# A two-branch linear-attention kernel rebuilt: small folds, V ahead of K, q's softmax in phase 1, tiles in pairs, an order listed by a planner

## The chip, the cores and the metric

One Trainium2 chip, one of its cores, one launch. The metric is device microseconds of an execution; the time is the median of some runs. TensorE (PE in the profile), VectorE (DVE), ScalarE (ACT), GpSimd (POOL) and the DMA queue of SyncE (SP) each work through their own list of instructions in order and wait for each other by semaphores.

## The reference

Two branches, A and B, with weights of their own, take the same x (2048 rows, 448 columns). A branch makes q, k and v for 16 heads of 28, maps q and k by a 28x28 matrix per head, and takes two softmaxes of each map, of the logits and of their negative, side by side. Then comes linear attention without a mask, an output projection, and a gate that mixes the branches:

```python
qkv = (x @ wqkv).reshape(B, S, 3, H, Dh) ...
pq = jnp.einsum("bhsd,hdf->bhsf", q, w_phi)
phi_q = jnp.concatenate([_softmax(pq, axis=-1), _softmax(-pq, axis=-1)], axis=-1)
...
kv = jnp.einsum("bhsf,bhsd->bhfd", phi_k, v)
z  = jnp.einsum("bhsf->bhf", phi_k)
num = jnp.einsum("bhqf,bhfd->bhqd", phi_q, kv)
den = jnp.einsum("bhqf,bhf->bhq", phi_q, z)[..., None] + 1e-6
o = num / den          # then  o @ wo
...
g = _sigmoid((x * gate_w).sum(-1, keepdims=True))
return g * a + (1 - g) * b
```

The two einsums kv and z sum over all rows, so nothing of num can start before the last tile of k.

## The kernel before

The rows are 16 tiles of 128. Every float32 matrix is held as a high and a low part (a rounded copy and the difference), and a product is made of the three terms that matter; that is why a projection of 448 inputs takes 11 matmuls a branch.

**Folds** (`fold`, L130). The map w_phi is multiplied into the weights of k and q at the start, as differences from the last feature, so that 27 columns a head remain and the 28th logit is zero. `fold` makes a chunk of 128 input rows with eight matmuls of 112x128 into a pair of PSUM banks; ACT makes the high part, DVE the low part. K's four chunks stand ahead of everything, q's four are made in tiles 2 to 5.

**Phase 1** (`for t in range(NT)`, L279). Per tile: `proj` of K (22 matmuls), `shift` (L161: DVE takes maximum and minimum of each head, subtracts for both signs; ACT takes the exponentials), `k_soft` (L175: DVE sums, reciprocal, POOL multiplies), `proj` of V (22 matmuls), `v_out` on ACT, and `kv_acc` (L196) of the tile before, 32 small matmuls that add kv and z into one PSUM bank. PSUM tiles of two banks rotate among three buffers (`two_tile`, L123). POOL splits x (L86) and wo (L251).

**The way of q.** `q_front` (L211) subtracts the maximum on DVE and writes the tile to DRAM with four transfers, then reads it back in another layout (32 tokens of four groups on the partitions). `q_exp0`, `q_min`, `q_exp1` (L229 to L239) make both exponentials there, undivided, and `q_turn` (L246) transposes them in blocks of 32 on DVE. q of tiles 0 to 3 goes through at the end of phase 1 and right after it, the rest in phase 2, four tiles ahead.

**The turn.** After phase 1, `kvs` is copied and transposed to `kvt`, wo is loaded into the place of K's weights (L340), and `gates` (L268) sends the last three tiles' gates through DRAM.

**Phase 2** (`for i in range(NT + 2)`, L437), an order written by hand. Per tile: `num` (L361: 64 matmuls of 32x32, the two signs kept apart, with a column of ones for the softmax's sums), q's projection of a later tile, `n_turn` (DVE transposes 2048 columns), `n_rec` and `n_mix` (reciprocals, products, gate and the sum of the signs; POOL, the last two tiles on DVE), `o_turn` (L400) with its low part (L410, L414), `out_mm` (L418: 21 matmuls) and the store. All transfers are issued by SP in the order of the code.

Of the kernel before, what the change touches and what calls it, by code (L numbers as in the profile page):

```python
# [8 lines left out]
F32 = mybir.dt.float32  # L9
# [16 lines left out]
HP = 32  # L26
WARM = 16
LEAD = 4
T0 = NT - 3
MID = 4  # L30


@with_exitstack
def hedgehog_mix(ctx: ExitStack, tc: tile.TileContext, xd, wv, wkt, wqt, wphi, wo, cmask, cpmask, out):
    nc = tc.nc
    ctx.enter_context(tc.manual_schedule())

    const = ctx.enter_context(tc.tile_pool(name="const", bufs=1))
    one_stack = ExitStack()
    one = one_stack.enter_context(tc.tile_pool(name="one", bufs=1, space=bass.MemoryType.PSUM))  # L40
    two_stack = ExitStack()
    two = two_stack.enter_context(tc.tile_pool(name="two", bufs=1, space=bass.MemoryType.PSUM))


    xg = [const.tile([P, 7, GT], F32R, name=f"xg{g}") for g in range(NG)]
    glog = const.tile([P, NT], F32, name="glog")
    gate = const.tile([P, 2, 4, NT], F32, name="gate")
    kvs = const.tile([P, 2, 2, 4, HP], F32, name="kvs")
    kvt = const.tile([P, 2, 2, 4, HP], F32, name="kvt")
    work = ctx.enter_context(tc.tile_pool(name="work", bufs=2))  # L50
    dram = ctx.enter_context(tc.tile_pool(name="dram", bufs=1, space=bass.MemoryType.DRAM))
# [4 lines left out]
    qd = [dram.tile([4, 32, 4, 8 * DH], F32, name=f"qd{i}") for i in range(2)]  # L56
    ph = ctx.enter_context(tc.tile_pool(name="ph", bufs=2))
    wp_ = ctx.enter_context(tc.tile_pool(name="wts", bufs=1))

    res = ctx.enter_context(tc.tile_pool(name="res", bufs=1, side="right"))  # L60
    wtb = res.tile([P, 4096], F32, name="wtb")
    xrb = res.tile([P, 2048], F32, name="xrb")
    start = ExitStack()
    raw = start.enter_context(tc.tile_pool(name="raw", bufs=1, side="right"))
    ident = raw.tile([P, P], F32, name="ident")
    make_identity(nc, ident)
    mask = raw.tile([PF, 4], F32, name="mask")
    wp = raw.tile([PF, 2, 4, HP], F32, name="wp")
    wpd = raw.tile([PF, 2, 4, FD], F32, name="wpd")
    bd = wp_.tile([PF, 2, 4, 4 * FD], F32, name="bd")  # L70
    wkh = wp_.tile([P, 4, 2 * FW], F32R, name="wkh")
    wkl = wp_.tile([P, 4, 2 * FW], F32R, name="wkl")
    wvh = wp_.tile([P, 4, VC], F32R, name="wvh")
    wvl = wp_.tile([P, 4, VC], F32R, name="wvl")
    NV = 2
    vs = [ph.tile([P, 2, NP, 2, DH + 1], F32, name=f"vs{i}", bufs=1) for i in range(NV)]
# [16 lines left out]
    def load_wt(src, n):
        wt = wtb[:PF].rearrange("p (b g c) -> p b g c", b=2, g=4)
        for c in range(0, 512, n):
            for b in range(2):
                nc.sync.dma_start(wt[:, b, :, c:c + n], src[b, :, c:c + n].rearrange("(g p) c -> p g c", p=PF))
        return wt

    def load_wv(c):  # L100
        wvr[c] = raw.tile([P, VC], F32, name=f"wvr{c}")
        nc.sync.dma_start(wvr[c], wv[c * P:(c + 1) * P, :])

    def split_w(wr, wh, wl, eng):
        nc.scalar.activation(wh, wr, AF.Copy)
        eng.tensor_tensor(wl, wr, wh.bitcast(F32), OP.subtract)  # L106

    nc.sync.dma_start(wp, wphi)
    nc.sync.dma_start(mask, cmask)
    wt = load_wt(wkt, 128)  # L110
    load_x(0, 0, P)
    for c in range(4):
        load_wv(c)
    load_x(0, P, 2 * P, GT)
    for v in vs:
        nc.gpsimd.memset(v[:, :, :, :, DH:], 1.0)
    nc.vector.tensor_tensor(wpd, wp[:, :, :, :FD], wp[:, :, :, FD:DH].to_broadcast([PF, 2, 4, FD]), OP.subtract)
    for q in range(4):
        nc.vector.tensor_scalar(bd[:, :, :, q * FD:(q + 1) * FD], wpd, mask[:, q:q + 1], None, op0=OP.mult)
    twos = [two.tile([P, 2, 512], F32, name=f"two{i}") for i in range(3)]  # L120
    turn_of = [0]

    def two_tile():  # L123
        turn_of[0] += 1
        return twos[turn_of[0] % 3]

    for ps in twos:
        nc.vector.memset(ps[:, :, FZ:FZ + H], 0.0)

    def fold(c, wt, wh, wl):  # L130
        ps = two_tile()
        for b in range(2):
            for g in range(4):
                nc.tensor.matmul(ps[:, b, g * 4 * FD:(g + 1) * 4 * FD], wt[:, b, g, c * P:(c + 1) * P], bd[:, b, g],  # L134
                                 start=True, stop=True)
        dh = wh[:, c, :].rearrange("p (b f h) -> p b f h", b=2, f=FD)
        dl = wl[:, c, :].rearrange("p (b f h) -> p b f h", b=2, f=FD)
        src = ps[:, :, :FW].rearrange("p b (h f) -> p b f h", f=FD)
        nc.scalar.activation(dh, src, AF.Copy)
        nc.vector.tensor_tensor(dl, src, dh.bitcast(F32), OP.subtract)  # L140

    def proj(t, wh, wl, widths, ps, at=0):
        x = xg[t // 4]
        o = (t % 4) * P
        lo = 0
        for b, n in enumerate(widths):
            terms = [(c, wh, c) for c in range(3)] + [(4 + c, wh, c) for c in range(3)]
            terms += [(3, wh, 3)] + [(c, wl, c) for c in range(4)]
            for i, (xc, w, wc) in enumerate(terms):
                nc.tensor.matmul(ps[:, b, at:at + n], x[:, xc, o:o + P], w[:, wc, lo:lo + n],  # L150
                                 start=i == 0, stop=i == len(terms) - 1)
            lo += n
        return ps
# [4 lines left out]
    def fm(ps):  # L158
        return ps[:, :, FO:FO + D].rearrange("p b (f h) -> p b h f", h=H)

    def shift(ps):  # L161
        p4 = fm(ps)
        mx = ph.tile([P, 2, 2, H], F32, name="mx")
        e = ph.tile([P, 2, HA * DH], F32, name="e")
        nc.vector.tensor_reduce(mx[:, 0], p4, AX.X, OP.max)  # L165
        nc.vector.tensor_reduce(mx[:, 1], p4, AX.X, OP.min)
        e5 = e.rearrange("p s (b h f) -> p s b h f", b=2, f=DH)
        bc = [mx[:, s, :, :, None].to_broadcast([P, 2, H, DH]) for s in range(2)]
        nc.vector.tensor_tensor(e5[:, 0], p4, bc[0], OP.subtract)  # L169
        nc.vector.tensor_tensor(e5[:, 1], bc[1], p4, OP.subtract)  # L170
        for s in range(2):
            nc.scalar.activation(e[:, s], e[:, s], AF.Exp)  # L172
        return e

    def k_soft(e):  # L175
        sm = ph.tile([P, 2, HA], F32, name="sm")
        rs = ph.tile([P, 2, HA], F32, name="rs")
        for s in range(2):
            nc.vector.tensor_reduce(sm[:, s], e[:, s].rearrange("p (h f) -> p h f", f=DH), AX.X, OP.add)  # L179
# [4 lines left out]
        return e

    def v_out(t, ps):
        v = vs[t % NV]
        nc.scalar.activation(v[:, :, :, :, :DH].rearrange("p b j q f -> p b (j q) f"), hb(ps[:, :, :D]), AF.Copy)
        nc.scalar.activation(glog[:, t:t + 1], ps[:, 0, D:D + 1], AF.Copy)


    kvb = one.tile([P, 512], F32, name="one")
    nc.vector.memset(kvb, 0.0)
    kvp = kvb[:, :HA * DH // 2].rearrange("p (b g s f) -> p b g s f", b=2, g=4, f=DH)

    def kv_acc(t, phi):  # L196
        v = vs[t % NV]
        for b in range(2):
            for g in range(4):
                for r in range(4):  # L200
# [8 lines left out]
    def q_front(k, ps):  # L211
        seq[k] = len(seq) % 2
# [13 lines left out]
    def tview(k):  # L226
        return tq[seq[k]].rearrange("p c b g f -> p (b g) c f")
# [282 lines left out]
```

## Time and profile before

| what | value |
|---|---|
| median of 3 runs | 393.68 us (393.07 to 394.75) |
| the profiled execution | 395.19 us |
| its span, first to last instruction | 393.4 us |
| mean granted PE clock | 0.965 |
| bytes moved by DMA | 38.5 MB |

The profile is of one execution. Busy time counts what an engine spends in instructions; a stage view gives it for stretches of the span. Matmuls are counted by passes, and a plain float32 one has two: 64 matmuls of `num` are 128 records. In a group's row stand the line, the engine, the operation, the output and input, the shapes, the count, then busy us and mean ns of one, then the idle time before them. The chain that ended last is followed back from the last instruction; its rows have start, length and what.

### The profile page before, as it was taken

How to read it: one execution, taken by the hardware profiler on the slowest of the kernel's cores; microseconds unless marked ns; L12 is line 12 of the kernel's file. 1: busy time of each engine (PE TensorE's matmuls, PEld its weight loads, DVE VectorE, ACT ScalarE, POOL GpSimd, SP SyncE). 2: the span in 40 equal slices, each digit the busy share in tenths (PEclk: the TensorE clock that was granted, in tenths of full speed). 3: DMA queues.
4: the chain of work that ended last, by engine and by line, in shares of the span. 5: the costliest groups of instructions: out<-in, count | busy, mean ns of one | idle time of the engine just before them, and what ended most of it. 6: DMA issues, size and time to landing. Idle time of an engine off the chain costs nothing.

```text
span 393.4 us, 10387 instructions
## 1 busy us (share of the span) xinstructions
PE 355.6 (90%) x4608; PEld 320.0 (81%) x4608; DVE 294.4 (75%) x326; ACT 122.8 (31%) x174; POOL 220.7 (56%) x182
## 2 busy tenths in 40 slices
PE   5999999999999999999965179999999999997765
PEld 5999999999999999999963069888888888875554
DVE  2676767666666667669743299999999999998991
ACT  1744353233333333222410032332233333332112
POOL 0184816375444444313400399988888988889311
PEclk9999999999999999999987588999999999999989
DMA  8928411100222222131158133444434334420001
GB/s 183 311 65 271 184 49 56 53 25 26 90 69 68 69 68 69 25 96 47 48 140 351 28 97 93 118 120 118 118 80 149 76 102 121 118 95 25 27 23 47
DMA packets 27217, 38.52 MB, mean 98 GB/s; under 512 B 3732, under 2 KB 21892, under 8 KB 26884
## 3 DMA queue, kind: packets, MB, share of 16 engines
q1 hardware_dynamic: 27172, 37.85, 31.9%
q8 instruction: 36, 0.59, 0.6%
q14 instruction: 9, 0.07, 0.1%
HBM read 23.62 MB, written 15.84 MB: 100 GB/s over the span
## 4 chain that ended last, share of the span: by engine, by line
PE 71%; DVE 10%; DMA 8%; POOL 4%; issue 2%; SPq 2%; ACT 2%; POOLq 0%; DVEq 0%; ACTq 0%
PE two L150 33%; PE out L423 14%; PE q L150 12%; PE num L367 5%; PE two L134 4%; PE one L203 3%; DMA gd<-glog 3%; POOL xrb L235 2%; DMA tq<-qd 2%; DMA qd<-uq 2%; DVE wtb L247 1%; SPq L223 1%; DVE wvh L373 1%; DVE wvl L373 1%; DVE qmx L216 1%
## 5 line engine op out<-in xcount | busy, mean ns | idle before, releaser
L183 POOL TENSOR_TENSOR e<-e,rs 128x896 f32<-128x896 f32 x32 | 53.9, 1706 | 64.9 <-DVE rs L180 64.9
L423 PE MATMUL out<-wkh,e 128*128 128x448 f32 x224 | 52.4, 372 | 10.9 <-ACT bd L428 6.5
L172 ACT ACTIVATE e<-e 128x896 f32<-128x896 f32 x32 | 30.2, 954 | 97.5 <-DVE e L169 97.4
L423 PEld LDWEIGHTS out<-wkh,e 128*128 128x128 f32 x224 | 41.7, 189 | 16.8 <-ACT bd L428 8.0
L150 PE MATMUL q<-wqh,xg 128*128 128x432 f32 x168 | 41.6, 391 | 13.9 <-DVE uq L218 8.9
L150 PE MATMUL two<-wvh,xg 128*128 128x450 f32 (+1 forms) x224 | 50.8, 365 | 0.0
L150 PE MATMUL two<-wkh,xg 128*128 128x432 f32 x224 | 50.7, 365 | 0.0
L150 PEld LDWEIGHTS q<-wqh,xg 128*128 128x128 f32 x168 | 33.3, 204 | 18.2 <-DVE uq L218 9.4
L165 DVE TENSOR_REDUCE mx<-two 128x32 f32<-128x896 f32 x16 | 17.5, 1091 | 38.2 <-PE two L150 38.2
L150 PEld LDWEIGHTS two<-wvh,xg 128*128 128x128 f32 x224 | 42.1, 188 | 3.2
L150 PEld LDWEIGHTS two<-wkh,xg 128*128 128x128 f32 x224 | 40.9, 188 | 2.9 <-POOL xg L91 0.2
L235 POOL TENSOR_TENSOR xrb<-qmn,tq 128x896 f32<-128x896 f32 x16 | 28.2, 1762 | 23.5 <-DVE qmn L234 19.8
L247 DVE STREAM_TRANSPOSE wtb<-xrb 128x2048 f32<-128x2048 f32 x16 | 36.9, 2305 | 3.1 <-ACT xrb L239 3.1
L367 PE MATMUL num<-wtb,kvt 32*32 32x128 f32 x2048 | 31.6, 285 | 4.9 <-issue 2.5
L367 PEld LDWEIGHTS num<-wtb,kvt 32*32 32x32 f32 x2048 | 25.0, 104 | 11.8 <-issue 7.0
L179 DVE TENSOR_REDUCE sm<-e 128x32 f32<-128x896 f32 x32 | 33.3, 1080 | 1.1
L406 ACT ACTIVATE e<-turn 128x512 fp32r<-128x512 f32 x16 | 9.6, 599 | 69.8 <-DVE turn L403 69.8
L150 PE MATMUL two<-wvl,xg 128*128 128x450 f32 (+1 forms) x128 | 31.3, 365 | 0.0
L150 PE MATMUL two<-wkl,xg 128*128 128x432 f32 x128 | 30.6, 360 | 0.0
L423 PE MATMUL out<-wkl,e 128*128 128x448 f32 x112 | 26.4, 377 | 0.0
L373 DVE STREAM_TRANSPOSE wvh<-num 128x2048 f32<-128x2048 f32 x8 | 18.4, 2306 | 10.4 <-PE num L367 10.4
L150 PEld LDWEIGHTS two<-wvl,xg 128*128 128x128 f32 x128 | 24.0, 188 | 2.3 <-POOL wvl L106 0.4
(95 smaller groups left out, 623.5 us busy)
## 6 DMA issues: line engine op xcount, KB each, us to landing
tq<-qd SPq DMA_DIRECT2D x16, 448.0 KB
qd<-uq SPq DMA_DIRECT2D x36, 112.0 KB
out<-bd SPq DMA_DIRECT2D x16, 224.0 KB
wod<-wtb SPq DMA_DIRECT2D x14, 224.0 KB
qd<-wvh SPq DMA_DIRECT2D x28, 112.0 KB
xrb<-in_xt SPq DMA_DIRECT2D x3, 1024.0 KB
wvr<-in_wv SPq DMA_DIRECT2D x4, 449.0 KB
wtb<-in_wkt SPq DMA_DIRECT2D x8, 224.0 KB
```

What stands on the lines that cost most here:

```text
L134: nc.tensor.matmul(ps[:, b, g * 4 * FD:(g + 1) * 4 * FD], wt[:, b, g, c * P:(c + 1) * P], bd[:, b, g], start=True, stop=True)
L150: nc.tensor.matmul(ps[:, b, at:at + n], x[:, xc, o:o + P], w[:, wc, lo:lo + n], start=i == 0, stop=i == len(terms) - 1)
L165: nc.vector.tensor_reduce(mx[:, 0], p4, AX.X, OP.max)
L172: nc.scalar.activation(e[:, s], e[:, s], AF.Exp)
L179: nc.vector.tensor_reduce(sm[:, s], e[:, s].rearrange("p (h f) -> p h f", f=DH), AX.X, OP.add)
L183: nc.gpsimd.tensor_tensor(e3, e3, rs[:, s, :, None].to_broadcast([P, HA, DH]), OP.mult)
L203: nc.tensor.matmul(kvp[32 * r:32 * r + DH + 1, b, g], v[:, b, h // 2, h % 2], phi[:, :, hs:hs + DH], start=(t == 0 and b == 0 and g == 0), ...
L235: nc.gpsimd.tensor_tensor(eq[:, 1, :, :, :DH], mn.rearrange("p c a -> p a c")[:, :, :, None].to_broadcast([P, 8, 4, DH]), tview(k), OP.sub ...
L247: nc.vector.transpose(e_slot(k), eq.rearrange("p s a c f -> p (s a c f)"))
L367: nc.tensor.matmul(ps[32 * g:32 * g + 32, r, 2 * b + s], kvt[32 * r:32 * r + 32, b, s, g], eTs[i][32 * r:32 * r + 32, s, b, g], start=True ...
L373: nc.vector.transpose(cb[i % 2][:, :2048], ps.rearrange("p r a t -> p (r a t)"))
L423: nc.tensor.matmul(ps[:, :D], a, w, start=n == 0, stop=n == len(terms) - 1)
```

## The change

The kernel is written anew around a planner. `Plan` takes each step with an engine, a cost in us, keys that it reads and writes, and emits the steps in the order of a simulated run: at each moment the engine that is free first takes, among what is ready, the step whose due time is earliest. TensorE's order is that of the list `steps()`. The costs are written into the code; what the chip does with them is not fed back.

- **Folds:** per branch 64 matmuls of 32x32 with 128 columns into all four banks of one PSUM tile, one DVE transpose of 2048 columns, then high and low parts by quarters.
- **Start:** x of two tiles (512 KB) and the first branch's V weights (four pieces of 230 KB) are loaded ahead of K's (eight of 230 KB); V of tiles 0 and 1 is made before the first fold. x comes in pairs of tiles (256 columns), three pairs kept.
- **PSUM:** two tiles of four banks in place of the rotating ones. K has two banks, V two, q two, kv one, each of them single.
- **K's softmax:** DVE subtracts for one sign; ACT copies the logits to SBUF (`pk`) and POOL subtracts for the other. The sums' reciprocals are taken per sign.
- **q's softmax:** `q_soft` sums both exponentials, takes reciprocals and multiplies on POOL before the transpose, through one buffer (`eq`). Tiles 0 to 9 have it in phase 1; tiles 0 to 7 are then kept in DRAM (`spill`, 1 MB each) and read back (`fetch`) in phase 2; tiles 10 to 15 have it in phase 2.
- **num:** with q divided by its sums, the two signs add in PSUM; two tiles share one transpose and one reciprocal. The column of ones is gone.
- **mix:** one product with the gated reciprocal and one for the output, on POOL; the last pair on DVE.
- **Phase 2:** eight pairs of tiles; the out matmuls of a pair follow num of the next.

The diff, cut to its core, added lines only (the old functions they replace are those above):

```diff
+                    f = free.get(eng, 0.0)
+                    if eng == "SP" and len(flight) >= 8:
+                        f = max(f, flight[-8])
+                    t = max(f, min(ready[i] for i in c))
+                    if best is None or t < best[0]:
+                        best = t, eng
+            t, eng = best
+            i = min((i for i in can[eng] if ready[i] <= t), key=lambda i: due[i])
+            can[eng].remove(i)
+            _, cost, lat, _, _, kb = self.steps[i]
...
+    yield from (("V", 0, 0), ("V", 1, 0), ("V", 0, 1), ("FK", 0), ("V", 1, 1), ("FK", 1), ("x1",), ("V", 2), ("x", 2))
+    yield from (("K", 0), ("wq", 0), ("wq", 1), ("FQ", 0), ("V", 3), ("FQ", 1), ("later",), ("K", 1), ("wo_rows",), ("V", 4))
+    yield from (("K", 2), ("Q", 0), ("S", 0, 0), ("kv", 0, 1), ("V", 5), ("K", 3), ("Q", 1), ("S", 1, 1))
+    for p in range(2, 8):
+        if p < 7:
+            yield "x", p + 1
+        yield "K", 2 * p
+        yield "Q", 2 * p - 2
+        if 2 * p - 2 < JIT:
+            yield "S", 2 * p - 2, 0
+        yield "kv", 2 * p - 2, 2 * p - 1
+        yield "wo", p - 2
+        if p in (3,):
+            yield "wo", 6
+        if p < 6:
...
+    yield from (("load_wo",), ("V", 14), ("V", 15), ("free_v",), ("gates", 12, NT), ("Q", 13), ("kv", 14, 15), ("free_e",), ("kv_turn",))
+    yield from (("fetch", 0, 2), ("fetch", 1, 3), ("Q", 14))
...
+    for p, (tiles, slots) in enumerate(pairs):
+        yield "num", tiles, slots
+        if p == 0:
+            yield from (("Q", 15), ("free_x",))
+        if p:
+            for i, t in enumerate(pairs[p - 1][0]):
+                yield "out", 2 * p - 2 + i, t, (2, 0)[i]
+        end = p == len(pairs) - 1
+        yield "mix", p, ("DVE", "DVE") if end else ("POOL", "POOL"), (3, 1), ("DVE", "DVE") if end else ("POOL", "POOL")
+        if p + 2 < len(pairs):
+            for t, s in zip(*pairs[p + 2]):
...
+JIT = 10
+SPILL = list(range(JIT - 2))
...
+    def fold(b, wh, wl, key, low):
+        def mm():
+            for g in range(4):
+                for o in range(4):
+                    for q in range(4):
+                        nc.tensor.matmul(t1[32 * o:32 * o + 32, q, g * P:(g + 1) * P], wpd[32 * q:32 * q + DH, b, g],
+                                         wt[b][32 * q:32 * q + DH, g].rearrange("p (j o i) -> p o j i", o=4, i=32)[:, o],
+                                         start=True, stop=True)
+        banks = [("t1", i) for i in range(4)]
...
+        put("DVE", 2 * D, lambda: V.tensor_reduce(mx[:, 0], p4, AX.X, OP.max), kb, [km[0]])
+        put("DVE", 2 * D, lambda: V.tensor_reduce(mx[:, 1], p4, AX.X, OP.min), kb, [km[1]])
+        put("ACT", 2 * D, act(pk, t0[:, :2, FO:FO + D]), kb, [("pk",)])
+        put("DVE", 2 * D, tt("DVE", e5[:, 0], p4, bc[0], OP.subtract), [*kb, km[0]], [ke[0]])
+        put("POOL", 2 * D, tt("POOL", e5[:, 1], bc[1], fm(pk), OP.subtract), [("pk",), km[1]], [ke[1]])
         for s in range(2):
             e3 = e[:, s].rearrange("p (h f) -> p h f", f=DH)
...
+            put("ACT", 2 * D, act(e[:, s], e[:, s], AF.Exp), [], [ke[s]])
+            put("DVE", 2 * D, lambda s=s, e3=e3: V.tensor_reduce(sm[:, s], e3, AX.X, OP.add), [ke[s]], [("sm", t % 2, s)])
+            add("DVE", 0.25, lambda s=s: V.reciprocal(sm[:, s], sm[:, s]), [], [("sm", t % 2, s)])
+            put("POOL", 2 * D, tt("POOL", e3, e3, sm[:, s, :, None].to_broadcast([P, 2 * H, DH]), OP.mult), [("sm", t % 2, s)], [ke[s]])
+
...
+    def q_soft(k, slot):
+        i = k % 2
+        tq, kt, ke = tqs[i], ("tq", i), [("eq", 0), ("eq", 1)]
+        add("SP", 0.4, dma(tq.rearrange("p c b g f -> p (c b g f)"), qd[k].rearrange("r t c x -> (r t) (c x)")),
+            [("qd", k, c) for c in range(4)], [kt], lat=2.6, kb=640)
+        tv = tq.rearrange("p c b g f -> p (b g) c f")
+        put("ACT", 2 * D, act(eq[:, 0, :, :, :DH], tv, AF.Exp), [kt], [ke[0]])
+        put("DVE", 2 * D, lambda: V.tensor_reduce(qmn, tq.rearrange("p c b g f -> p c (b g) f"), AX.X, OP.min), [kt], [("qmn",)])
+        put("POOL", 2 * D, tt("POOL", eq[:, 1, :, :, :DH], qmn.rearrange("p c a -> p a c")[:, :, :, None].to_broadcast([P, 8, 4, DH]), tv, OP.subtract),
+            [kt, ("qmn",)], [ke[1]])
+        put("ACT", 2 * D, act(eq[:, 1, :, :, :DH], eq[:, 1, :, :, :DH], AF.Exp), [], [ke[1]])
+        for s in range(2):
+            e3 = eq[:, s].rearrange("p a c f -> p (a c) f")[:, :, :DH]
+            put("DVE", 2 * D, lambda s=s, e3=e3: V.tensor_reduce(qsm[:, s], e3, AX.X, OP.add), [ke[s]], [("qsm", s)])
+            add("DVE", 0.25, lambda s=s: V.reciprocal(qsm[:, s], qsm[:, s]), [], [("qsm", s)])
+            put("POOL", 2 * D, tt("POOL", e3, e3, qsm[:, s, :, None].to_broadcast([P, 2 * H, DH]), OP.mult), [("qsm", s)], [ke[s]])
...
+    def spill(k, slot):
+        add("SP", 0.4, dma(ed[k], eTf[slot]), [("eT", slot)], [("ed", k)], lat=3, kb=1048)
+
+    def fetch(k, slot):
+        add("SP", 0.4, dma(eTf[slot], ed[k]), [("ed", k)], [("eT", slot)], lat=3, kb=1048)
...
+    def num(p, tiles, slots):
+        nt = len(tiles)
+        def go():
             for b in range(2):
...
+                for i in range(nt):
+                    for s in range(2):
+                        for g in range(4):
+                            for r in range(4):
+                                o = (b * nt + i) * P
+                                nc.tensor.matmul(t0[32 * g:32 * g + 32, r, o:o + P], kvt[32 * r:32 * r + 32, b, s, g],
+                                                 eTs[slots[i]][32 * r:32 * r + 32, s, b, g],
+                                                 start=(b == 0 and i == 0 and s == 0), stop=s == 1, skip_group_check=True)
+        banks = [("t0", i) for i in range(4)]
+        add("PE", 0.4 + 1.95 * nt, go, [("kvt", 0), ("kvt", 1), *[("eT", s) for s in slots]], banks)
```

More of the change, by code (lines that the diff above doesn't have):

```diff
@@ L36, in hedgehog_mix @@
     ctx.enter_context(tc.manual_schedule())
[L38 to L47, printed above, removed]
@@ L55, in hedgehog_mix @@
     gd = dram.tile([P, NT], F32, name="gd")
[L56 to L64, printed above, removed]
@@ L93, in load_wt @@
[L93 to L106, printed above, removed]
@@ L120, in hedgehog_mix @@
[L120 to L131, printed above, removed]
-        for b in range(2):
[L133 to L153, printed above, removed]
+    qd = [dram.tile([4, 32, 4, 8 * DH], F32, name=f"qd{i}") for i in range(NT)]
@@ L158, in fm, with v_proj @@
     def fm(ps):
[L159 to L166, printed above, removed]
+        return ps.rearrange("p b (f h) -> p b h f", h=H)
+    def v_proj(t, b):
+        o, n = ((0, D + 2), (VB, D))[b]
+        w = [x[:, :, o:o + n] for x in (wvh, wvl)]
+        k = b if t == 1 else 2 + b
+        add("PE", 11 * 0.203, mms(t, w, t0[:, k, :n]),
+            xkeys(t) + [("v" + h, c, b) for h in "hl" for c in range(4)], [("t0", k)])
+        v = vs[t % NV]
+        put("ACT", D, act(v[:, b, :, :, :DH].rearrange("p j q f -> p (j q) f"), t0[:, k, :D].rearrange("p (h f) -> p h f", f=DH)),
+            [("t0", k)], [("v", t % NV, b)])
+        if b == 0:
+            add("ACT", 0.2, act(glog[:, t:t + 1], t0[:, k, D:D + 1], AF.Exp, scale=-1.0), [("t0", k)], [("gl", t)])
@@ L184, in k_soft @@
[L184 to L197, printed above, removed]
-        for b in range(2):
-            for g in range(4):
-                for r in range(4):
-                    h = 4 * r + g
-                    hs = (b * H + h) * DH
-                    nc.tensor.matmul(kvp[32 * r:32 * r + DH + 1, b, g], v[:, b, h // 2, h % 2],
-                                     phi[:, :, hs:hs + DH], start=(t == 0 and b == 0 and g == 0), stop=(t == NT - 1),
-                                     skip_group_check=True)
@@ new lines, in warm, with first @@
+    def warm():
+        for _ in range(WARM):
+            nc.tensor.matmul(t0[:, 3, :P], zero, zero, start=True, stop=True)
+    def first(eng, cost, fn, w):
+        add(eng, cost, fn, [], w)
+    first("DVE", 0.1, lambda: V.memset(zero, 0.0), [("zero",)])
+    add("PE", WARM * 0.2, warm, [("zero",)], [("t0", 3)])
+    load_x(0)
+    for b in range(2):
+        for c in range(4):
+            load_wv(c, b)
+        if b == 0:
+            load_wp()
+    for b in range(2):
+        load_wt(wkt, b)
+        if b == 0:
+            split_x(0, 0, P, "DVE")
+            split_x(0, P, 2 * P, "POOL")
+            load_x(1)
```

655 lines of the change are left out of this document (377 added, 278 removed).

## The prediction

> **What bounds the kernel now.** I read the page first, then the stages, then the chain that ended last, then the groups of each engine. The page's busy line shows which engine leads:
>
> ```profile
> PE 355.6 (90%) x4608; PEld 320.0 (81%) x4608; DVE 294.4 (75%) x326; ACT 122.8 (31%) x174; POOL 220.7 (56%) x182
> ```
>
> PE is busy for nine tenths of the span. An average hides stages with other limits, so the next view is busy time by stage (stretch, length, busy us and instructions of each engine, granted clock, DMA share, GB/s):
>
> ```profile
> core 0: us, PE busy (x) PEld busy (x) DVE busy (x) ACT busy (x) POOL busy (x), PEclk, DMA share, GB/s
> 0.00:4.50 4.50, 0.00 (x0) 0.02 (x1) 1.64 (x9) 0.01 (x1) 0.84 (x8) 1.00 0.46 123
> ...
> 14.80:160.00 145.20, 145.20 (x1510) 133.02 (x1513) 102.26 (x107) 56.39 (x77) 73.68 (x47) 1.00 0.27 90
> ...
> 201.00:242.00 41.00, 24.61 (x450) 21.36 (x451) 21.98 (x26) 5.77 (x7) 18.19 (x19) 0.71 0.49 160
> 242.00:342.00 100.00, 100.00 (x1562) 89.53 (x1560) 95.53 (x108) 33.13 (x48) 87.78 (x78) 1.00 0.39 106
> 342.00:393.40 51.40, 36.94 (x640) 30.35 (x638) 39.28 (x44) 12.22 (x21) 25.51 (x22) 0.96 0.15 49
> ```
>
> The reader is to see two solid stretches, 15 to 160 and 242 to 342, in which PE never stops at full clock, and three bad ones: the start, the turn between the phases (24.6 of 41 us busy, at clock 0.71), and the tail (36.9 of 51.4). In the first stretch DVE is at 70% and POOL at 51%; in the second they are at 96% and 88%. The work is badly spread: vector engines have room in phase 1 and none in phase 2.
>
> The chain that ended last (start, us, what) prices each piece of PE work and names what fills the turn:
>
> ```profile
> 7.88 7.13 PE two L134 x64
> ...
> 54.82 1.77 PE two L134 x16
> ...
> 109.71 0.92 PE one L203 x64
> 110.63 9.01 PE two L150 x44
> ...
> 208.19 11.61 DMA gd<-glog
> ...
> 248.37 4.54 PE q L150 x22
> 252.91 4.26 PE out L423 x21
> 257.17 1.83 PE num L367 x102
> ...
> 389.97 0.54 ACT bd L428
> ```
>
> So a tile costs PE 9.01 us for K and V, 0.92 for the kv sums, 4.54 for q, 1.83 for num and 4.26 for out: 20.56, by 16 tiles 329.0. The folds take 7.13 for K and 4 x 1.77 for q: 14.2. Work at full pace is 343.2 of the span of 393.4; **50 us are start, turn and tail**. In the turn a gate of 1.5 KB waits 11.61 us behind the two loads of wo, and POOL waits with it.
>
> **The change part by part.** *PE work.* V, K, q, kv, num and out keep their matmuls (the two signs of num add into one PSUM area, so there are still 64 a tile). A fold becomes 64 matmuls of 32x32 with 128 columns, which is the shape and count of num: 4 x 1.83 = 7.3 in place of 14.2. Nothing here shows that a strided moving operand runs as fast; the ends are 1.83 and 7.13 each, and I take the row of the same shape. PE's floor is 329.0 + 7.3 = **336.3**.
>
> *Start.* Now x and the first half of wv are loaded ahead of K's weights, 512 KB and 920 KB. The rows for what DMA needs (first a piece of the chain, then a stretch of the view by stage on PE alone, whose last figure is GB/s):
>
> ```profile
> 0.72 2.02 DMA wp<-in_wphi
> ```
> ```profile
> 10.00:15.00 5.00, 5.00 (x46) 1.00 1.10 344
> ```
> ```profile
> 200.00:205.00 5.00, 3.41 (x11) 0.70 0.64 166
> ```
>
> First data land 2 us after the issue at 0.7; 1.43 MB at 344 GB/s is 4.2 us more; V of tile 0 starts near 7 us. Behind it stand two more V halves and the first fold, 6.7 + 1.8 us, while the rest (4 MB at that rate: 12 us) arrives, so PE should run on. The warm-up matmuls end about 3 us before, and a pause of that length at 198 to 201 is followed by a stretch at clock 0.70: a loss of 1.5 us in 5. I charge 7 + 2 = **9** (ends 7 and 13, the second if wv lands at 233 GB/s, the rate of the first slices, with the splits behind it).
>
> *Phase 1, the q softmax added.* DVE's rows, with two starts that show the true spacing of such operations, and the means of groups in both solid stretches:
>
> ```profile
> 105.27 1.09 DVE L165 TENSOR_REDUCE mx<-two 128x32 f32<-128x896 f32 x1 [3.08 <-PE two L150]
> 106.28 1.08 DVE L166 TENSOR_REDUCE mx<-two 128x32 f32<-128x896 f32 x1
> ```
> ```profile
> L179 DVE TENSOR_REDUCE sm<-e 128x32 f32<-128x896 f32 x27 | 28.1, 1081 | 1.1
> ```
> ```profile
> L247 DVE STREAM_TRANSPOSE wtb<-xrb 128x2048 f32<-128x2048 f32 x10 | 23.0, 2302 | 0.0
> ...
> L234 DVE TENSOR_REDUCE qmn<-tq 128x32 f32<-128x896 f32 x10 | 10.3, 1030 | 0.0
> L216 DVE TENSOR_REDUCE qmx<-q 128x32 f32<-128x896 f32 x10 | 10.3, 1029 | 0.0
> ...
> L403 DVE STREAM_TRANSPOSE turn<-vs 128x512 f32<-128x512 f32 x10 | 7.1, 711 | 0.0
> L412 DVE TENSOR_TENSOR e<-turn,e 128x512 fp32r<-128x512 f32 x10 | 6.8, 681 | 0.0
> L218 DVE TENSOR_TENSOR wvh<-q,qmx 128x448 f32<-128x448 f32 x10 | 5.8, 620 | 0.2
> ...
> L389 DVE RECIPROCAL cden<-cden 128x32 f32<-128x32 f32 x10 | 3.1, 310 | 0.0
> L382 DVE RECIPROCAL crs<-wvl 128x64 f32<-128x64 f32 x5 | 2.8, 554 | 0.2
> L404 DVE STREAM_TRANSPOSE wvh<-vs 128x384 f32<-128x384 f32 x5 | 2.7, 539 | 0.0
> ```
> ```profile
> L172 ACT ACTIVATE e<-e 128x896 f32<-128x896 f32 x28 | 26.5, 954 | 78.7 <-DVE e L169 78.6
> L188 ACT ACTIVATE vs<-two 128x896 f32<-128x896 f32 x14 | 12.6, 901 | 0.0
> ```
>
> A K tile on DVE: maximum and minimum 1.0 each, one subtraction 1.08 (the other goes to POOL), two sums 2.16, two reciprocals 0.62: 5.86. q's front: 1.03 + 2 x 0.62 = 2.27. q's softmax: minimum 1.03, sums 2.16, reciprocals 0.62, transpose 2.30: 6.11. Together 14.24, against PE's 9.01 + 0.92 + 4.54 = 14.47 a tile: DVE is at 98% while ten tiles have their softmax in phase 1. One new thing eats the rest. POOL's subtraction needs a copy (pk) that ACT makes out of the same PSUM banks from which DVE takes maximum and minimum; no row here has both engines on one PSUM tile. If the copy slips between DVE's reads in turn, DVE stands 0.90 us and two hand-overs, 1.0 a tile, and what is listed behind the minimum, q's front among it, stands with it: 15.24, and ten tiles lose 7.7. If both read at once it costs nothing. I take **8** of this phase's waits, the upper end, since DVE and PE are that close; ends 0 and 16 (the same us on all sixteen K tiles).
>
> [...]
>
> Loads and stores move too: spills and fetches add 16 MB, and each is behind q's own transfers on SP; at the 106 GB/s of phase 2 and a share of 0.39 the 16 DMA engines cover that.
>
> *Turn.* wo is loaded as soon as K's weights are done, under V of tiles 14 and 15, q of 13, kv, q of 14: 9.0/2 x 2 + 4.54 + 0.92 x 2 + 4.54 = 20 us of PE against the 11.61 us for which those loads held the queue. What is left late is q of tile 15, whose PSUM waits for a front that waits for DMA: **3** (ends 0 and 11.6).
>
> *Phase 2, in pairs.* PE: 2 x (4.26 + 1.83) = 12.18 a pair. DVE: one softmax 6.11, num's transpose 2.30 for two tiles (half as much data a tile, the signs being added), reciprocal 0.55, output turns 2 x (0.71 + 0.54 + 0.68): 12.82. POOL's rows:
>
> ```profile
> L235 POOL TENSOR_TENSOR xrb<-qmn,tq 128x896 f32<-128x896 f32 x10 | 17.7, 1765 | 3.1 <-issue 3.1
> ...
> L397 POOL TENSOR_TENSOR vs<-wvh 128x896 f32<-128x896 f32 x5 | 10.6, 2121 | 0.4
> ...
> L416 POOL TENSOR_TENSOR e<-wvl,e 128x384 fp32r<-128x384 f32 x5 | 5.1, 1018 | 0.0
> ```
>
> POOL: 3 x 1.77 + 2 x (0.27 + 1.77 to 2.12) + 2 x 1.02 = 11.4 to 12.1; I take 1.77, since the mix has a broadcast operand as L235 has. Six pairs carry a softmax, so DVE costs 6 x 0.64 = **4**. With three engines at 94 to 105% some waits won't be covered; the stretch 242 to 342 shows none at 96 and 88%. I add 0.8 a pair, **5** (ends 0 and 12).
>
> *Tail.* In the last pair num, transpose, reciprocal and DVE's mix run beside the two outs of the pair before (8.5 us); after the last matmul come ACT's copy and the store, 3.4 us as from 389.97 to 393.4 now.
>
> *Sum.* 9 + 336.3 + 3.4 = 348.7; + 8 + 3 + 4 + 5 = 368.7 of span. The profiled execution took 395.19 for a span of 393.4, so 370.5; the median shown, 393.68, is 1.5 below that execution: **369**.
>
> **The rivals.** *B, PE paces everywhere.* Reads of one bank don't wait and the cover holds as in 242 to 342: 348.7 + 3 gives about 352; with half the waits 360. For: PE at 100.00 of 100 now with DVE at 96%. Against: DVE's sums of 14.24 and 12.82 leave no room.
>
> *C, DVE paces.* Besides the copy, DVE, which works in listed order, stands while ACT makes the two exponentials (2 x 0.95) that each pair of sums follows. That is 15.24 + 1.9 = 17.1 a tile, 2.7 above PE, 27 us for ten tiles: 348.7 + 27 + 12 = 388. For: nothing off PE has room left. Against: there is other DVE work to list in between, and the lead of some us that PE's other banks allow.
>
> *D, slower than before: the single buffer of q's softmax.* All sixteen tiles pass through one buffer: POOL 1.77, ACT 0.95, DVE 1.08 + 0.31, POOL 1.77, DVE 2.30, in all 8.2 us plus five hand-overs, each behind what its engine has listed ahead. If a turn takes c us, PE pays 10 x (c - 14.47) + 6 x (c - 12.18). It decides the sign when this reaches 393.7 - 348.7 - 3 = 42 us, at c = 16.2; that is 1.6 us lost at each of the five. At c = 16.6 the time is about 400. The rows of one such chain now (ACT's second exponential, then the transpose):
>
> ```profile
> 275.45 0.95 ACT L239 ACTIVATE xrb<-xrb 128x896 f32<-128x896 f32 x1 [0.26 <-POOL xrb L235]
> ...
> 277.48 2.30 DVE L247 STREAM_TRANSPOSE wtb<-xrb 128x2048 f32<-128x2048 f32 x1
> ```
>
> The transpose starts 1.08 us after its input, in a DVE that is 96% full. At about 1 us for each of five, c is 13: under 14.47, a little over 12.18. So D is unlikely, yet the order is fixed by listed costs, and one late engine holds the others.
>
> **How the numbers follow.** The forecast, 361 to 379, has 0.50; B, below that, 0.15; C, 379 to 391.7, 0.20; no change 0.04; D 0.11. This kernel's measurement tells 0.5%, some 2 us, from no change. Faster is 0.85, same 0.04, slower 0.11. The range leaves out D, no change and the lowest end of B: 353 to 392.
>
> **What would show it.** PE above 95% in every slice from 10 us to the last five; no slice at 200 to 242 with a lower clock; PE busy near 336 + 4 us; DVE's share above 80%; ACT's pk copy and DVE's minimum starting one after the other (or at once: B). C shows as PE waiting for K's subtraction or q's front on DVE; D as DVE waiting for POOL's products in the softmax and PE at less than 85% from 60 to 190. I am wrong in kind if folds take over 3 us each, or if PE waits on DMA in the middle.

## The result: 462 us, a sixth slower

The changed kernel takes 461.94 us (median of 4 runs, 461.66 to 462.91) beside 393.85 us for the kernel before: a ratio of 1.173, 95% interval 1.170 to 1.176. The forecast was 369.0 with a range of 353 to 392, so even the sign is wrong. The profiled execution took 461.99 us for a span of 460.2. Of the kernels below, e9, e10 and e11 have runs over 1.5% longer than their fastest: medians are of all runs, ratios and intervals leave those out.

First the page's busy line, with PE and its granted clock in 40 slices:

```profile
PE 379.6 (82%) x5012; PEld 328.8 (71%) x5012; DVE 298.8 (65%) x363; ACT 144.9 (31%) x219; POOL 250.9 (55%) x182
...
PE   8787677988899889889989977788885958859765
...
PEclk9999876999999999999999996979998879888979
```

No engine is full: PE has fallen from 90% to 82%, DVE from 75% to 65%. Work that waits in turn looks like this, not work that one engine bounds. By stage (stretch, length, busy us and instructions of each engine, granted clock, DMA share, GB/s):

```profile
24.00:90.00 66.00, 51.47 (x669) 43.54 (x639) 37.91 (x39) 26.22 (x39) 26.53 (x18) 0.87 0.32 98
90.00:255.00 165.00, 150.25 (x1316) 132.62 (x1315) 131.05 (x160) 62.88 (x86) 120.05 (x72) 1.00 0.41 139
255.00:300.00 45.00, 36.35 (x391) 31.83 (x390) 29.66 (x39) 10.03 (x15) 23.39 (x15) 0.87 0.38 132
300.00:428.00 128.00, 101.29 (x2335) 87.09 (x2334) 82.78 (x100) 29.91 (x53) 70.26 (x59) 0.89 0.31 103
428.00:460.20 32.20, 20.86 (x84) 17.72 (x84) 10.52 (x15) 4.95 (x11) 0.99 (x1) 0.88 0.10 36
```

The two solid stretches of before are gone. PE stands in every row: 14.5 us in 24 to 90, 14.8 in 90 to 255, 8.7 in the turn, 26.7 in phase 2, 11.3 in the tail. Over the span PE's idle time went from 37.8 to 80.6 us and its busy time from 355.6 to 379.6: 42.8 + 24.0 = the 66.8 us between the spans. What PE waits for (reader <- releaser: us in all, times, longest; "t" is either of the two four-bank tiles, since the profile leaves numbers out):

```profile
PE t L518 <- DVE rx L238: 15.0, 5, 5.6
PE t L338 <- ACT vs L241: 14.5, 14, 4.5
PE t L338 <- ACT glog L241: 9.5, 12, 1.8
PE t L471 <- issue: 8.4, 6, 1.8
PE t L518 <- ACT re L241: 5.3, 3, 2.1
```

L338 is a projection, L471 `num`, L518 an output, and L238 and L241 are helpers that DVE or POOL, and ACT, go through. Two of these rows make no sense by banks. `vs` and `glog` are ACT's reads of **V's** banks, but of the 24.0 us of waits for them 20.7 stand before the matmuls of **K** (weights `rk`), in other banks:

```profile
L338 PE MATMUL t<-rk,rx 128*128 128x432 f32 x352 | 82.1, 387 | 21.9 <-ACT vs L241 11.9 <-ACT glog L241 8.8 <-DVE re L238 1.2
```

One such place in the timeline (start us, length, engine, line, out<-in, then the idle time before it and its releaser):

```profile
162.78 4.71 PE L338 MATMUL t<-rv,rx 128*128 128x450 f32 x22
...
167.53 0.55 ACT L241 ACTIVATE vs<-t 128x448 f32<-128x448 f32 x1 [0.81 <-PE t L338]
167.97 0.17 ACT L241 ACTIVATE glog<-t 128x1 f32<-128x1 f32 x1
...
168.19 2.43 PE L338 MATMUL t<-rk,rx 128*128 128x432 f32 x11 [0.69 <-ACT glog L241]
...
170.66 0.55 ACT L241 ACTIVATE vs<-t 128x448 f32<-128x448 f32 x1 [1.68 <-PE t L338]
171.25 2.43 PE L338 MATMUL t<-rk,rx 128*128 128x432 f32 x11 [0.63 <-ACT vs L241]
```

Read it as a ping-pong. V is complete at 167.49, both halves. ACT copies the first (bank 2) and the gate's column; only then may K's first half (bank 0) start. ACT's copy of V's second half (bank 3), long complete, then stands 1.68 us until K's first half has ended; and K's second half stands until that copy is done. Nobody needs any of it: the four accesses are in four places. What they share is the PSUM **tile** `t0`. The same in the tail, where outputs are in banks 2 and 0 of `t1` and DVE's turn in 3 and 1:

```profile
428.78 0.54 ACT L241 ACTIVATE re<-t 128x448 f32<-128x448 f32 x1 [0.35 <-DVE rx L238]
429.38 4.55 PE L518 MATMUL t<-rk,rx 128*128 128x448 f32 x21 [2.15 <-ACT re L241]
434.02 0.73 DVE L506 STREAM_TRANSPOSE t<-rv 128x512 f32<-128x512 f32 x1 [1.09 <-PE t L518]
434.80 4.54 PE L518 MATMUL t<-rk,rx 128*128 128x448 f32 x21 [0.88 <-DVE t L506]
```

Output, turn, output: each ends before the next begins. In each of these places the releaser that the profile names is an engine that has just used another bank of the same tile.

**The theory (T)**: the waits that are generated order accesses of different engines to one allocated PSUM tile, whatever banks they touch. By this the two four-bank tiles cost the loss, and cutting them up takes it away. **The rivals**: banks are what counts and the loss is in the listed order and its costs, in the ACT copy `pk` that alternates with DVE (P), or in the loads of wo that hold up the start (W). By those, cutting up the tiles changes little.

### The profile page after: what moved, and what is told of

Its sections match the earlier page's. It is cut to its first block, busy times and chain, and to the rows that moved or that the text cites. A ratio compares the mean times of both kernels' runs of the same rounds, so it can differ in the third digit from the quotient of the medians.

```text
span 460.2 us, 11405 instructions
## 1 busy us (share of the span) xinstructions
PE 379.6 (82%) x5012; PEld 328.8 (71%) x5012; DVE 298.8 (65%) x363; ACT 144.9 (31%) x219; POOL 250.9 (55%) x182
## 5 line engine op out<-in xcount | busy, mean ns | idle before, releaser
L518 PE MATMUL t<-rk,rx 128*128 128x448 f32 x336 | 83.0, 411 | 24.9 <-DVE rx L238 15.0
L338 PE MATMUL t<-rk,rx 128*128 128x432 f32 x352 | 82.1, 387 | 21.9 <-ACT vs L241 11.9
L518 PEld LDWEIGHTS t<-rk,rx 128*128 128x128 f32 x336 | 72.1, 218 | 35.1 <-DVE rx L238 14.0
L338 PE MATMUL t<-rv,rx 128*128 128x450 f32 (+1 forms) x352 | 83.2, 392 | 13.2 <-DVE mx L375 3.3
L338 PEld LDWEIGHTS t<-rk,rx 128*128 128x128 f32 x352 | 68.7, 201 | 34.7 <-ACT vs L241 16.4
L338 PEld LDWEIGHTS t<-rv,rx 128*128 128x128 f32 x352 | 69.4, 202 | 24.4 <-issue 10.8
L338 PE MATMUL t<-rq,rx 128*128 128x432 f32 x352 | 75.2, 370 | 4.6 <-DVE ru L238 3.9
L338 PEld LDWEIGHTS t<-rq,rx 128*128 128x128 f32 x352 | 67.8, 194 | 9.5 <-DVE ru L238 4.8
L238 POOL TENSOR_TENSOR re<-re,sm 128x896 f32<-128x896 f32 x32 | 53.9, 1705 | 35.0 <-DVE sm L384 35.0
L238 POOL TENSOR_TENSOR rt<-rt,qsm 128x896 f32<-128x896 f32 x32 | 54.1, 1705 | 15.3 <-DVE qsm L432 15.3
L431 DVE TENSOR_REDUCE qsm<-rt 128x32 f32<-128x896 f32 x32 | 33.1, 1055 | 19.0 <-ACT rt L241 18.9
L238 POOL TENSOR_TENSOR rt<-qmn,ru 128x896 f32<-128x896 f32 x16 | 28.2, 1761 | 29.1 <-DVE rt L434 19.7
L238 POOL TENSOR_TENSOR re<-mx,pk 128x896 f32<-128x896 f32 x16 | 35.5, 2216 | 14.7 <-DVE mx L376 14.7
L241 ACT ACTIVATE re<-re 128x896 f32<-128x896 f32 x32 | 30.3, 953 | 39.8 <-DVE re L238 31.8
L238 POOL TENSOR_TENSOR rx<-xraw,rx 64x256 fp32r<-64x256 f32 (+3 forms) x16 | 19.9, 1241 | 32.1 <-ACT rx L241 31.1
L241 ACT ACTIVATE vs<-t 128x448 f32<-128x448 f32 x32 | 17.4, 546 | 62.7 <-PE t L338 55.7
L383 DVE TENSOR_REDUCE sm<-re 128x32 f32<-128x896 f32 x32 | 33.3, 1075 | 4.2 <-ACT re L241 4.2
L241 ACT ACTIVATE re<-t 128x448 f32<-128x448 f32 x16 | 8.6, 542 | 86.9 <-PE t L518 64.9
L434 DVE STREAM_TRANSPOSE rt<-rt 128x2048 f32<-128x2048 f32 x13 | 29.7, 2288 | 0.0
L241 ACT ACTIVATE pk<-t 128x896 f32<-128x896 f32 x16 | 14.7, 918 | 44.9 <-DVE mx L375 23.7
L238 DVE TENSOR_TENSOR re<-t,mx 128x896 f32<-128x896 f32 x16 | 17.3, 1082 | 13.7 <-ACT glog L241 4.8
```

What stands on the lines that cost most here:

```text
L238: return lambda: ENG[eng].tensor_tensor(o, a, b, op)
L241: return lambda: A.activation(o, i, f, **k)
L338: nc.tensor.matmul(ps, x[:, xc, o:o + P], w[l][:, c], start=i == 0, stop=i == len(XT) - 1)
L383: put("DVE", 2 * D, lambda s=s, e3=e3: V.tensor_reduce(sm[:, s], e3, AX.X, OP.add), [ke[s]], [("sm", t % 2, s)])
L431: put("DVE", 2 * D, lambda s=s, e3=e3: V.tensor_reduce(qsm[:, s], e3, AX.X, OP.add), [ke[s]], [("qsm", s)])
L434: add("DVE", 2.25, lambda: V.transpose(eTf[slot], eq.rearrange("p s a c f -> p (s a c f)")), ke, [("eT", slot)])
```

## The experiments

Kernels are timed beside the kernel before on the same chip (medians 394.0 to 395.1 us there).

### Cut the tiles up: e1, e2, e3

Both tiles become six: K in a tile of two banks, V in two tiles of one bank, q in two banks, and two single banks for kv, turns and outputs. A transpose over four banks becomes three instructions. The order of the list stays, but turns and outputs go to other banks (cut):

```diff
-    t0 = psum.tile([P, 4, 512], F32, name="t0")
-    t1 = psum.tile([P, 4, 512], F32, name="t1")
+    tk = psum.tile([P, 2, 512], F32, name="tk")
+    tv = [psum.tile([P, 512], F32, name=f"tv{i}") for i in range(2)]
+    tq2 = psum.tile([P, 2, 512], F32, name="tq2")
+    tm = [psum.tile([P, 512], F32, name=f"tm{i}") for i in range(2)]
...
-                yield "out", 2 * p - 2 + i, t, (2, 0)[i]
+                yield "out", 2 * p - 2 + i, t, (2, 3)[i]
...
-        yield "mix", p, ("DVE", "DVE") if end else ("POOL", "POOL"), (3, 1), ("DVE", "DVE") if end else ("POOL", "POOL")
+        yield "mix", p, ("DVE", "DVE") if end else ("POOL", "POOL"), (0, 1), ("DVE", "DVE") if end else ("POOL", "POOL")
```

> The two four-bank PSUM tiles become six tiles (a pair of banks for K, one bank each for the two V halves; a pair for q, one bank each for the rest); the out matmuls move to banks 2 and 3 and the output turns to 0 and 1; the two big transposes become three instructions each. All else as in the changed kernel. Theory T (accesses by different engines to one PSUM tile are ordered one after the other, whatever their banks, so PE waits for readers of banks that it does not write): most of the loss goes, 365 to 390 us, and the waits of K's matmuls for V's copies and of V's for K's subtraction disappear. Rival R (the listed order and its lean costs, or the single buffer of q's softmax, hold everything): 440 us or more. Rival S (start and turn, and the clock after pauses): 440 to 455.

e2 cuts up only `t0`, e3 only `t1`.

> Only the first four-bank tile (K, V, num) is split. T: phase 1 loses its waits between K and V, some 30 to 40 us, phase 2 stays: 420 to 432 us. R: no change, 455 to 465.

> Only the second four-bank tile (q, kv, folds, output turns and outs) is split. T: phase 2 loses the waits of the out matmuls for the other tile's turn and copies, some 35 to 50 us, and its low clock; phase 1 stays: 412 to 428 us. R: no change, 455 to 465.

| kernel | median us | ratio to before (95%) | less than the change |
|---|---|---|---|
| e1, both | 387.89 | 0.982 (0.978 to 0.987) | 74.1 |
| e2, `t0` alone | 431.71 | 1.094 (1.091 to 1.097) | 30.2 |
| e3, `t1` alone | 421.85 | 1.068 (1.066 to 1.070) | 40.1 |

All three lie in the ranges that T gave. The two parts, 30.2 and 40.1, add up to 70.3 of the 74.1 us. The other banks for turns and outputs are in e1 and e3 alone, so they have no part in e2's 30.2. Each takes away its own waits and leaves the other's. What PE waits for longest in e2, where `t1` is still one tile:

```profile
PE t L529 <- DVE rx L243: 14.6, 5, 5.6
```

and in e3, where `t0` is still one:

```profile
PE t L349 <- ACT vs L246: 12.3, 14, 3.5
...
PE t L349 <- ACT glog L246: 9.5, 12, 1.8
```

In e1 neither is left. Its busy line, and its stage from 90 to 250:

```profile
PE 351.3 (92%) x5012; PEld 317.8 (83%) x5012; DVE 302.0 (79%) x387; ACT 143.8 (37%) x219; POOL 250.8 (65%) x182
```
```profile
90.00:250.00 160.00, 153.86 (x1475) 143.21 (x1475) 146.85 (x179) 66.45 (x90) 127.79 (x76) 0.99 0.45 146
```

The rest of the rebuilt kernel was not what was slow: with the same instructions, but for the cut transposes, it is 1.8% faster than the kernel before. PE is busy for 153.86 of those 160 us with DVE at 146.85, close to what the prediction had.

### The other way: e4, the kernel before with its three buffers in one tile

```diff
-    twos = [two.tile([P, 2, 512], F32, name=f"two{i}") for i in range(3)]
+    two_all = two.tile([P, 3, 2, 512], F32, name="two")
+    twos = [two_all[:, i] for i in range(3)]
```

> The kernel before, with its three rotating PSUM tiles of phase 1 allocated as one tile of three pairs of banks; no other edit. T: PE's projections must take turns with DVE's and ACT's reads of the other pairs: each of 16 tiles loses about 4.2 us to K's reads by DVE and 1 us to V's copy, so 60 to 90 us more, 455 to 480. R: no change, 393 to 396.

536.06 us, ratio 1.360 (1.356 to 1.363): the sign is T's, the size is not; 141 us were lost where 60 to 90 were expected. Its busy line:

```profile
PE 403.8 (76%) x4608; PEld 352.9 (66%) x4608; DVE 295.2 (55%) x326; ACT 123.7 (23%) x174; POOL 220.4 (41%) x182
```

its longest wait of PE, and the place in the timeline:

```profile
PE two L151 <- DVE e L171: 67.4, 16, 4.3
```
```profile
149.22 1.09 DVE L166 TENSOR_REDUCE mx<-two 128x32 f32<-128x896 f32 x1 [4.68 <-PE two L151]
150.22 1.08 DVE L167 TENSOR_REDUCE mx<-two 128x32 f32<-128x896 f32 x1
151.22 1.08 DVE L170 TENSOR_TENSOR e<-two,mx 128x896 f32<-128x896 f32 x1
152.22 1.08 DVE L171 TENSOR_TENSOR e<-mx,two 128x896 f32<-128x896 f32 x1
...
153.35 3.00 PE L151 MATMUL two<-wvh,xg 128*128 128x450 f32 x7 [4.17 <-DVE e L171]
```

V goes into another buffer than K, yet it stands while DVE reads K four times, 4.2 us, on each of the 16 tiles: 67.4 us, the size I had reckoned with. In the kernel before PE runs on during these reads: from 14.8 to 160 us it is busy for 145.20 of 145.20. I had left out the second part, PE at a lower clock (0.83 from 90 to 255 us of e4; 1.00 from 14.8 to 160 in the kernel before): PE's idle time grew by 92.0 us (37.8 to 129.8), its busy time by 48.2 (355.6 to 403.8) for the same matmuls.

### The copy pk: e5, e8, e9, e10

e5 is e1 without the copy; DVE subtracts for both signs, out of PSUM:

```diff
-        put("ACT", 2 * D, act(pk, tk[:, :, FO:FO + D]), kb, [("pk",)])
...
-            put("POOL", 2 * D, tt("POOL", e5[:, 1], bc[1], fm(pk), OP.subtract), [("pk",), km[1]], [ke[1]])
+            put("DVE", 2 * D, tt("DVE", e5[:, 1], bc[1], p4, OP.subtract), [*kb, km[1]], [ke[1]])
```

> The kernel with six PSUM tiles (E1), without the copy pk: DVE subtracts for both signs out of PSUM, as before the change. That adds one DVE operation of 1.08 us a tile (17 us in all) and takes away 2.2 us of POOL, 0.9 us of ACT and DVE's wait for the copy a tile. Theory P (the wait costs about 1 us a tile, as the prediction had it, and DVE is the bound of phase 1): within 3 us of E1. Rival (the copy costs nothing, since it fills holes): 8 to 15 us slower than E1.

406.46 us, 1.032 (1.027 to 1.037): 18.6 slower than e1, more than either theory gave. DVE's own work grew by 12.6 us (302.0 to 314.6). The longest of PE's waits there:

```profile
PE tm L410 <- POOL re L248: 11.0, 7, 2.5
```

The kv sums now wait for POOL's products, and POOL's wait for DVE's sums has grown from 20.6 us in e1 to 32.1. In this order, then, the subtraction on POOL pays for the copy. The planner orders all steps anew after such an edit, so the 18.6 us aren't the price of the copy alone.

e9 is e6 (below) with the copy listed ahead of DVE's reads, so that it no longer falls between them:

```diff
+            put("ACT", 2 * D, act(pk, tk[:, :, FO:FO + D]), kb, [("pk",)])
+            kb = [*kb, ("pk",)]
             put("DVE", 2 * D, lambda: V.tensor_reduce(mx[:, 0], p4, AX.X, OP.max), kb, [km[0]])
             put("DVE", 2 * D, lambda: V.tensor_reduce(mx[:, 1], p4, AX.X, OP.min), kb, [km[1]])
-            put("ACT", 2 * D, act(pk, tk[:, :, FO:FO + D]), kb, [("pk",)])
```

> E6 with the copy pk listed ahead of DVE's maximum, minimum and subtraction, which are told to wait for it, so that the planner gives DVE other work in that time. Theory P (DVE stands for the copy between its own reads, 10.1 + 2.6 us in E6, and DVE paces the end of phase 1): 4 to 12 us faster than E6. Rival (those waits lie in holes): within 3 us of E6.

It came out 404.0 us, 1.014 of before (1.010 to 1.019), where 4 to 12 us less than e6's 383.3 was expected: a miss, by the two ratios 16 us slower than e6. e10 is e9 with the planner's costs set to durations of the traces (DVE 0.06 us + 1.10 ns an element, reciprocal 0.33, POOL's subtraction 2.55 in place of 2 units).

> E9 with the planner's costs nearer to the profile: DVE 0.06 + 1.10 ns an element, its small reciprocal 0.33, its transposes 2.33 and 0.22 + 1.15 a tile, POOL's subtraction from pk 2.2 us. Theory O (the listed order does not fit since DVE is planned 5 to 10% too fast): 3 to 10 us faster than E9. Rival (the order holds anyway): within 3 us of E9.

395.74 us, 1.000 of before (0.996 to 1.003). By the two ratios the costs are worth 0.0146 x 394 = 5.8 us, in the range expected, and the order is still worse than e6's. Why the copy ahead of DVE's reads costs time is open.

### Later loads of wo, and more or fewer tiles in phase 1: e6, e7, e8, e11

e6 is e1 with the two transfers of 1.6 MB that put wo in order in DRAM held back until q's folds are done:

```diff
-            add("SP", 0.4, dma(w5[b], wo[b * D:(b + 1) * D, :].rearrange("(r g f) n -> g r (f n)", r=4, g=4)), [], [("wos", b)], lat=3, kb=1600)
+            add("SP", 0.4, dma(w5[b], wo[b * D:(b + 1) * D, :].rearrange("(r g f) n -> g r (f n)", r=4, g=4)), [("q", "h", 3, 1)], [("wos", b)], lat=3, kb=1600)
```

> E1 with the two DRAM-to-DRAM transfers of wo issued after q's folds are read, not between the loads of K's and q's weights. Theory W (these transfers hold the DMA queue, so that q's weights come late and all engines stand at 20 to 100 us): 8 to 16 us faster than E1, and q's second fold starts 10 us earlier. Rival (the start is held by the order of the other engines): within 3 us of E1.

383.30 us, 0.974 (0.969 to 0.979): **the fastest version measured, ahead of both kernels**. The gain over e1, 4.6 us by the medians and 3.4 by the ratios, is about half the smallest that W gave, and the two intervals just touch. W's other sign failed: the last matmul of q's second fold, which was to come 10 us earlier, starts at 50.5 us, and at 49.9 in e1. So that part of the start came no earlier, and where the few us come from is open.

e7 is e6 with `JIT = 12` in place of 10 (twelve tiles have q's softmax in phase 1), e11 with 8, e8 is e7 without pk, by the edit of e5.

> E6 with q's softmax of twelve tiles in phase 1 in place of ten (four in phase 2 in place of six; ten tiles kept in DRAM). If the softmax of late tiles holds num in phase 2: 4 to 10 us faster than E6. If phase 2 is held by the output's own steps, or phase 1's DVE has no room: within 3 us of E6, or slower.

> E7 without the copy pk. Theory P: within 3 us of E7, or slower by up to 8, since phase 1 then has two more softmaxes on DVE.

> E6 with q's softmax of eight tiles in phase 1 in place of ten, eight in phase 2. E7 with twelve was 19 us slower than E6. If DVE's load in phase 1 decides: faster than E6 by 3 to 12 us. If both phases are full, each in its own: slower than E6 by 3 to 15 us, as phase 2 gets 12 us more of DVE.

e7: 402.26 us, 1.018 (1.012 to 1.023). e8: 404.57, 1.026 (1.020 to 1.031). e11: 390.15, 0.984 (0.980 to 0.987). Both directions lose against e6, 17 to 19 and 4 to 7 us (by ratios and by medians), so ten is the best of the three. e7 was to gain 4 to 10 us if the late softmaxes held phase 2; it lost instead. e8 lies within 3 us of e7, as expected, and e11 is slower, as it was to be if both phases are full. In e7 the wait that e6 doesn't have is again that of kv:

```profile
PE tm L411 <- POOL re L248: 12.3, 5, 6.9
```

What is open: e5, e7, e8 and e9, four small edits of a list, all land at 402 to 406 by their medians. In e5, e7 and e8 PE's idle time is 44 to 46 us, and kv or K waits for POOL or DVE; why these lists leave such a gap and that of e6 doesn't, no run separates.

## Why the prediction was wrong, by its steps

**The step that failed.** The prediction took PSUM by banks. In the case against C it counted on "the lead of some us that PE's other banks allow", and in phase 1 it gave one wait between engines, that of `pk`. Its sum had no term for a wait between accesses to different banks, and none of its rivals had one. e1 to e3 show this term: 74 us, 30 in `t0` and 40 in `t1`; e4 shows the same in the kernel before. The change's own line, two tiles "in place of the rotating ones", was in the front of this document; no term of the sum and no rival comes from it.

**The rest of the miss** is read from e6, where this term is gone. Its profiled execution took 386.62 us, 3.3 more than its median. Its busy line, the row of PE's warm-up, and by a stage view of L307 alone the four folds (stretch, length, PE and PEld busy):

```profile
PE 352.1 (91%) x5012; PEld 315.6 (82%) x5012; DVE 302.5 (79%) x387; ACT 142.8 (37%) x219; POOL 251.2 (65%) x182
```
```profile
L549 PE MATMUL tv<-zero 128*128 128x128 f32 x36 | 5.8, 338 | 1.1 <-DVE zero L554 1.1
```
```profile
0.00:384.80 384.80, 11.27 (x512) 7.89 (x512) 0.97 0.45 144
```

PE's work without the warm-up is 352.1 - 5.8 = 346.3 us where the floor was 336.3, and all else is 384.8 - 346.3 = 38.5 of the span where 8 + 9 + 3 + 4 + 5 + 3.4 = 32.4 was put down. The 16.1 us over the forecast of 368.7 are 10.0 of work and 6.1 of waits. The work was **mis-sized** because each piece was priced at full clock: the kernel before showed it already, with 355.6 busy, of which 3.4 warm-up, for a sum of 343.2. The stretches of e6 at a lower clock are these (stretch, length, PE busy, clock, DMA share, GB/s):

```profile
24.80:28.20 3.40, 3.40 (x117) 0.50 0.91 183
38.40:45.20 6.80, 6.47 (x138) 0.50 0.38 142
89.60:96.40 6.80, 4.34 (x12) 0.50 0.25 84
270.50:277.40 6.90, 5.02 (x102) 0.51 0.86 283
```

PE is busy for 19.2 us in them. At full clock the same work would take about half (an estimate from the clocks of 0.50 and 0.51 in these rows), so most of the 10.0 us is the clock.

In the change itself the same two parts are 379.6 - 6.2 (warm-up) - 336.3 = 37.1 of work and 54.4 of waits.

**Folds.** The rate was right: a fold whose weights were there took 1.90 us for its 128 records, 1.83 were forecast. In e6 the four took 11.3 for a forecast of 7.3, in pieces between waits for weights and in part at half clock (0.50 from 24.8 to 28.2 us).

```profile
47.25 1.90 PE L297 MATMUL t<-rt,wpd 28*32 28x128 f32 x128
```

**Start.** V was to begin near 7 us; in the change it begins at 7.08.

**pk.** It was to alternate with DVE's reads, and does. DVE's waits in the change:

```profile
DVE mx L375 <- ACT pk L241: 12.9, 7, 2.9
...
DVE mx L376 <- ACT pk L241: 7.2, 7, 1.3
```

These are 20.1 us of DVE's time; the upper end for the whole kernel was 16, of PE's. A tile's copy costs DVE 1.26 us, where 1.0 was forecast. The 8 us of the sum rest on the two engines having to take turns at the same banks. No run shows that term: none lets both read at once, so what the chip would do isn't shown. In its place the runs showed these 20.1 us of DVE's time. What the copy costs PE stays open: without it the kernel is slower (e5), and with it first as well (e9).

**Durations on DVE** were right: 1055 and 1075 ns for the sums, 2288 for the transpose. One on POOL was not, the subtraction from the copy, 2216 ns where q's, of the same shape, took 1761:

```profile
L238 POOL TENSOR_TENSOR re<-mx,pk 128x896 f32<-128x896 f32 x16 | 35.5, 2216 | 14.7 <-DVE mx L376 14.7
L238 POOL TENSOR_TENSOR rt<-qmn,ru 128x896 f32<-128x896 f32 x16 | 28.2, 1761 | 29.1 <-DVE rt L434 19.7
```

**Signs named ahead.** Of what was to show the steps, PE above 95% from 10 us on and DVE above 80% failed at once (82 and 65% over the span), and the turn, now at 255 to 300, has clock 0.87. C did not come: PE waits little for q's front and K's subtraction. Nor did D: from 60 to 190 PE is busy for 113.86 of 130 us, 88% where D asked for less than 85, and no row shows DVE waiting for POOL's products.

```profile
PE t L338 <- DVE ru L238: 3.9, 3, 2.4
...
PE t L338 <- DVE re L238: 3.0, 3, 1.8
```
```profile
60.00:190.00 130.00, 113.86 (x1000) 99.68 (x999) 90.62 (x114) 47.59 (x68) 89.11 (x55) 0.96 0.37 126
```

## What to carry to other kernels

Before pricing the waits of a kernel, list for each allocated PSUM tile which engines access it, in program order. In the programs of this case such accesses went one after another even in different banks (74.1 us of the change's time, 67.4 us of PE's waits in e4), so allocate one tile for each thing that should run on its own, not one large tile for several. In a trace the sign is a matmul released by an engine that has just read something else, as K's by ACT's copy of V in the change (0.63 us at 171.25) and V's by DVE's subtraction for K in e4 (4.17 us). And price a stretch by PE's busy time as it was measured, clock included, not by its cleanest pieces.

## What the runs showed of the hardware

In e4 PE pauses once a tile before V's matmuls, 16 times and 67.4 us in all, and its clock from 90 to 255 us is 0.83. The matmuls of V's high part behind these pauses have a mean of 492 ns a record, 365 in the kernel before:

```profile
L151 PE MATMUL two<-wvh,xg 128*128 128x450 f32 (+1 forms) x224 | 74.9, 492 | 67.4 <-DVE e L171 67.4
```

Cut where the clock changes, one tile of e4, whose pause ends at 187.05, goes at half clock and then at full (stretch, length, PE busy, clock, DMA share, GB/s):

```profile
185.20:192.10 6.90, 5.05 (x14) 0.51 0.02 4
192.10:202.30 10.20, 7.53 (x96) 1.00 0.20 67
```

So the 5.05 us of work behind this pause would have been about half at full clock (an estimate from the two clocks, 0.51 and 1.00): the pause costs some 2.5 us on top of its length.

In the change the many short pauses do no such harm. From 90 to 255 us PE stands twenty times for 0.63 to 1.00 us, and the clock there is 1.00. The other stages, at 0.87 to 0.89, have longer pauses: 4.51 and 3.28 us from 24 to 90, 3.28 in the turn, up to 5.65 in phase 2, 3.64 in the tail. After the 4.51 us before K's matmuls at 53.66 the clock is 0.52, and 22 of them take 7.36 us; after a pause of 1.00 us the same 22 take 4.56:

```profile
53.66 7.36 PE L338 MATMUL t<-rk,rx 128*128 128x432 f32 x22 [4.51 <-ACT vs L241]
...
102.88 4.56 PE L338 MATMUL t<-rk,rx 128*128 128x432 f32 x22 [1.00 <-DVE re L238]
```
```profile
53.00:60.00 7.00, 6.34 (x18) 0.52 0.15 43
```

Where it begins can't be read from these runs: pauses of 1.68 and 1.82 us, each a few us behind another, have a slow stretch after them (at 394 and 73 us), and pauses of 2.03 and 2.15 us (before 327 and 429) have none.

So in these runs waits cost more than their length. In e4 92 us of added idle time came with 48 us of added work. The change, beside e1 with as many matmuls, has 48.2 us more idle time (80.6 and 32.4) and 28.3 us more work (379.6 and 351.3).
